# Eighteen weight-sum jobs in half 1 instead of twenty, two on VectorE beside the attention product, and a shorter preparation of half 2

## The chip, the cores and the metric

One core of a Trainium2 chip runs the whole program. TensorE (PE) multiplies matrices, VectorE (DVE), ScalarE (ACT) and GpSimd (POOL) work on tiles in on-chip memory, and SyncE (SP) issues transfers (DMAs); ACT and POOL issue some as well. Each engine takes its instructions in the order in which they stand, and waits where one isn't ready. Time is device time of one execution in microseconds (us); smaller is better.

## The reference

```
xn = layernorm(x)                               x: 2048 x 1024, f32
s  = linear attention of xn with wqkv (32 heads of 32), times wo
       phi(t) = where(t > 0, t + 1, exp(t)) + 1e-6
       o = phi(q) (phi(k)^T v) / (phi(q) sum(phi(k)) + 1e-6)
h  = silu(xn w1) * (xn w3)                      w1, w3: 1024 x 3584
out = x + s * silu(h w2)                        w2: 3584 x 1024
```

Both branches read xn.

## The kernel before

Every large product is made with fewer multiplications than the plain one, in f32 precision by three matmuls each (high times high, high times low, low times high, lines 109 to 111). So each operand is first split into a high part (ACT, line 103 or 474) and a low part (DVE, line 104 or 475).

**Halves.** The 2048 rows are worked on in two halves (`half(h)`). Half 1 (h = 0) makes keys, queries, then 14 pairs of hidden columns; half 2 (h = 1) makes keys and queries in turn, row products, then its 14 pairs. A pair is a gate gemm (`g0_8_` is that of pair 8 in half 1) and an up gemm (`u0_8_`). A gemm is seven products of 12 matmuls of 128x512, named by letter and operand: a with B11, b with T2, c with T3, d with T1, a again with B21, e with T4, d again with B22. They multiply the seven tiles A11, S2, S3, S1, A12, A22, S4 of the half's normalised rows, 2.1 MB each, always in that order. Half 2's seven tiles go into the places of half 1's, so each load (line 904, from `a_d`) waits until PE has done its last product with the old tile.

**Weights.** A pair's two weight blocks (1 MB each, line 442) go into two buffers in turn. Those of w1 and w3 are asked for by ACT, in its own instruction order, ahead of the cast of the block before; those of q and k by SP. All transfers of SP and ACT share eight completion semaphores in turn, so an issue waits until the transfer that had its semaphore before has landed.

**Side jobs.** `catch_up` is called after most products and lets one step of one side job be written there; `yield` ends a step. Side jobs, in this order: `prepare_next` (4 jobs: half 2's rows are normalised, transposed, combined and stored to `a_d`), then `weight_sums` (28 jobs): each loads eight blocks of w2 (line 1157), makes sums of them on POOL in three steps (11 instructions, tiles `w2s` and `w`, line 989) and stores them to `wt_d` by SP (line 1167), for the last product. Its tiles rotate through four buffers. `next_work` queues 20 of them in half 1, `attention_work` eight in half 2; what is left at the end of a half is written out at once. Every two pairs, sums of the hidden tiles (`hs`, `early_sums` and `later_sums`) go to POOL too, and to `h_d` by the queue in `stores_by`; while `later_sums` yields True, no weight sums step is written. ACT's next `h` tile (line 969) waits until these have read the old one.

**After half 2.** The attention product makes eight blocks of 256 rows, 84 matmuls each after the first (`tokens`): banks `as`, `bs`, `cs`, `ds`, emptied by DVE (lines 1455 to 1494), operands split one block ahead. Then the last product with h, `wt_d` and w2. A scheduler fixes the order of each engine from these program steps; `tc.issue_after` adds orders by hand.

Of the kernel before, what the change touches and what calls it, by code (L numbers as in the profile page):

```python
# [9 lines left out]
F32 = mybir.dt.float32  # L10
# [12 lines left out]
def tile_linear_attention_times_swiglu(  # L23
# [10 lines left out]
    nc = tc.nc  # L34
# [4 lines left out]
    NF = F // P  # L39
# [299 lines left out]
    def prepare_next(i):  # L339


        def turn(n, src):
            p_ = bank(f"t{n}1_{i}")
            for k in range(ND // 2):
                nc.tensor.transpose(p_[:, k * P:(k + 1) * P], src[:, k * P:(k + 1) * P], ident)
            return p_

        def steps(_):
            t = [job_tile([P, D], f"xn{i}_{e}") for e in range(2)]
            for c in range(2):  # L350
# [12 lines left out]
            bs = st.tile([P, 2, 2, nc.vector.BN_STATS_DIM], F32, tag="bs", name=f"bs1_{i}")  # L363
            for c in range(2):
                gather(t[c], bs[:, c])
                yield True
            spread(bs, m)
            yield True
            for c in range(2):
                normalise(t[c], m[:, c])  # L370
                yield True

            a11, a12, a21, a22 = (t[c][:, n * C:(n + 1) * C] for c in range(2) for n in range(2))
            keep_rows(1, i, "A11", t[0])
            keep_rows(1, i, "A22", a22)
            g = job_tile([P, 2, C], f"xg{i}")
            nc.vector.tensor_add(out=g[:, 0], in0=a21, in1=a22)
            yield True
            nc.vector.tensor_sub(out=g[:, 1], in0=a11, in1=a21)
            yield True  # L380
            keep_rows(1, i, "S1", g.rearrange("p n c -> p (n c)"))
            p_ = turn("A21", a21)
            nc.scalar.copy(out=a21, in_=p_)
            yield True
            yield True
            nc.vector.tensor_sub(out=g[:, 0], in0=g[:, 0], in1=a11)
            yield True
            nc.vector.tensor_sub(out=g[:, 1], in0=a12, in1=g[:, 0])
            yield True
            keep_rows(1, i, "S2", g.rearrange("p n c -> p (n c)"))  # L390
            p_ = turn("A11", a11)
            keep("A11", p_)
            nc.scalar.copy(out=a11, in_=p_)
            yield True
            p_ = turn("A12", a12)
            keep("A12", p_)
            nc.scalar.copy(out=a12, in_=p_)
            yield True
            p_ = turn("A22", a22)
            nc.scalar.copy(out=a22, in_=p_)  # L400
            yield True
            keep("A22", p_)
            yield True
            nc.vector.tensor_add(out=a22, in0=a21, in1=a22)
            yield True
            keep("S1", a22)
            yield True
            nc.vector.tensor_sub(out=a21, in0=a11, in1=a21)
            yield True
            keep("S3", a21)  # L410
            yield True
            nc.vector.tensor_sub(out=a11, in0=a22, in1=a11)
            yield True
            keep("S2", a11)
            yield True
            nc.vector.tensor_sub(out=a12, in0=a12, in1=a11)
            yield True
            keep("S4", a12)
            yield True

        return Job(lambda: None, steps)
# [163 lines left out]
    jobs = []  # L585
# [275 lines left out]
    def half(h):  # L861
        A = operand_tiles(h)

        def keys(pair, **how):
            return gemm(ops[f"k{h}_{pair}_"], A, uses[pair], **how)

        def run(g):
            for _ in g:
                pass

        def side_by_side(*gemms):
            for _ in zip_longest(*gemms):
# [12 lines left out]
        uses = [key_rows(h, pair) for pair in range(ND // 2)]  # L885
        if h == 0:
            early = [ops[f"k0_{pair}_"] for pair in range(ND // 2)]
            m = [keys(pair, early=True, own=pair == 0, led=pair == 0) for pair in range(ND // 2)]
            some = mybir.EngineType
            with tc.manual_schedule(engines={some.PE, some.Activation, some.DVE, some.Pool}):  # L890
                last = Opening(A, early, m).run()
            wide[0] = True
            for k in early[2:]:
                k.ask()
            early[2].then = early[3].next
        else:

            ops["q1_0_"].ask()
            for i, n in enumerate(AOPS):
                with ExitStack() as behind:  # L900
                    if i > 1:
                        behind.enter_context(tc.issue_after(ops["q1_0_"].asked.ins))
                    for k in range(ND // 2):
                        nc.sync.dma_start(out=A[n][:, :, k].bitcast(F32), in_=a_d[n][:, :, k])
        if h == 0:
            with tc.issue_after(last.ins):
                for g in m:
                    run(g)
        else:
            stores_by[0] = nc.gpsimd  # L910
            side_by_side(keys(0, paired=True), queries(0, paired=True))
            wide[0], stores_by[0] = True, nc.sync
            for pair in range(1, ND // 2):
                run(keys(pair))
                run(queries(pair))
            jobs.append((all_denominators(), False))
            for _ in row_products():
                pass
        jobs.append((attention_work(), False) if h else (next_work(), True))
        if h == 0:  # L920
            for pair in range(ND // 2):
                wide[0] = pair < ND // 2 - 1
                held[0] = 0 if wide[0] else HOLD
                run(queries(pair))
        wide[0] = False
        for pair in range(NF // 2):
            last = h < NH - 1 and pair == NF // 2 - 1
            gemms = [gemm(ops[f"{'gu'[e]}{h}_{pair}_"], A, use, paired=last) for e, use in enumerate(hidden(h, pair))]
            if last:
                side_by_side(*gemms)  # L930
            else:
                for g in gemms:
                    run(g)
        while jobs:
            run(jobs.pop(0)[0])
        if h:
            store_all()
            sums_by[0], stores_by[0] = nc.vector, nc.gpsimd

    def four_sums(x1, x2, s12, s34, e=nc.gpsimd):  # L940

# [127 lines left out]
    def later_sums(h, t, tiles, last):  # L1069
# [3 lines left out]
            keep_sums(h, t, q, pw0.tile([P, 2, 2, P], F32, tag="w0_6", name=f"hk{h}_{t}"))  # L1073
            yield True
        for i, _ in enumerate(steps):
            yield i < 6
            if last:
                yield True

# [64 lines left out]
        e.tensor_sub(out=b22, in0=b22, in1=b11)  # L1144
        e.tensor_sub(out=b21, in0=b21, in1=b22)

    def weight_sums(t, part, place=job_tile, queue=nc.sync):

        e = pool

        cols = slice(part * P, (part + 1) * P)

# [7 lines left out]
        def steps(r):  # L1160
            o1, o2 = (place([P, 8, P], f"w2s{t}_{part}_{i}") for i in range(2))

            def some(x, i, step):
                return x[:, i:i + step + 1:step]
# [12 lines left out]
            e.tensor_sub(out=o2[:, 3], in0=o1[:, 2], in1=r[:, 6])  # L1177
            e.tensor_sub(out=o2[:, 4:6], in0=some(r, 2, 3), in1=o1[:, 5:7])
            yield True
            e.tensor_sub(out=o2[:, 6:8], in0=some(o1, 4, 3), in1=r[:, 3:5])  # L1180
            store(8, o2)
            e.tensor_add(out=r[:, 0], in0=r[:, 1], in1=o2[:, 1])
# [4 lines left out]
        return Job(load, steps)  # L1187

    WSUMS = [(t, part) for t in range(NQ) for part in range(4)]
    NOW = 20  # L1190

    def next_work():

        yield from go_on([prepare_next(i) for i in range(TH // 2)])
        jobs.append((go_on([weight_sums(*w) for w in WSUMS[:NOW]]), "sums"))

    hm4 = const.tile([P, P // DH], F32, name="hm4")
    nc.vector.memset(hm4, 0.0)
# [171 lines left out]
    def attention_work():  # L1370
# [3 lines left out]
                work += key_values(k + e * (ND // 2)) + [j]  # L1374
        work += [divide(m, k) for m in range(2, S // (2 * P)) for k in range(ND // 2)]
        yield from go_on(work, 3)
        jobs.append((go_on([weight_sums(*w) for w in WSUMS[NOW:]]), "sums"))


    groups = []  # L1380
# [229 lines left out]
    jobs.clear()  # L1610
    pw0 = ctx.enter_context(tc.tile_pool(name="pw0", bufs=1, reuse_waits="tile"))

    ORDER = [p for chain in CHAINS for p in chain]
    STEPS = [(i, c) for i in range(len(ORDER)) for c in range(NCH)]
    OPENS, CLOSES = {c[0] for c in CHAINS}, {c[-1] for c in CHAINS}
# [157 lines left out]
```

## Time and profile before

| | |
|---|---|
| median of 3 runs | 2310.02 us (2305.24 to 2311.41) |
| profiled execution: time, span | 2305.8 us, 2304.0 us |
| busy share PE, DVE, ACT, POOL | 98%, 67%, 45%, 30% |
| mean granted TensorE clock | 0.995 |
| moved by DMA | 495.20 MB, 215 GB/s on the mean |
| weight sums on POOL | 472.7 to 1618.5 us (308 instructions, in both halves) |
| first matmul of half 2 | 748.0 us |

In rows of the profile stand the start and the duration in us, the engine, the line, the tiles as out<-in and a count; a bracket tells how long the engine had stood idle before and what ended it. An engine's name with q (SPq, ACTq) is its queue issuing a transfer; a row that begins "DMA" after the times is a transfer itself. Windows give busy us of each engine with the count of instructions, then the granted TensorE clock (1.00 is full), the share of the DMA engines and GB/s. A matmul's row shows a duration longer than the distance to the next, since matmuls overlap; counts in a window tell the rate.

### The profile page before, as it was taken

The numbers are of one execution on the slowest core, as the hardware profiler recorded it, in microseconds if no ns is written. First come the engines' busy times: TensorE is split into PE (matmuls) and PEld (weight loads), VectorE is DVE, ScalarE is ACT, GpSimd is POOL, SyncE is SP. The second block draws the span as 40 slices with busy tenths as digits, with TensorE's granted clock in tenths as the row PEclk, the third lists the DMA queues.
The fourth block names the chain that finished last, engine by engine and source line by source line (L and its number), as shares of the span: only waits on it lengthen the run. The fifth ranks groups of instructions, "written<-read, shape, count | busy, mean of one in ns | idle before, by whom it ended". The sixth has DMA issues, their size and how long they took to land.

```text
span 2304.0 us, 31463 instructions
## 1 busy us (share of the span) xinstructions
PE 2259.7 (98%) x10584; PEld 1847.6 (80%) x10584; DVE 1549.4 (67%) x2571; ACT 1041.8 (45%) x1778; POOL 702.6 (30%) x1171
## 2 busy tenths in 40 slices
PE   7999999999998899999999999999999999999998
PEld 6888888888877688777788888888888888888887
DVE  8987777666544686555866688865865555566576
ACT  6655544444332455433444444343623544444452
POOL 2220324367776522000332454477221000001010
PEclk9999999999999999999999999999999999999999
DMA  6555556577778745777765667777766756668595
GB/s 243 177 184 169 177 160 194 181 212 222 200 218 268 289 153 171 249 240 247 214 212 162 208 203 242 247 210 222 244 215 190 263 197 210 224 218 266 193 302 203
DMA packets 449842, 495.20 MB, mean 215 GB/s; under 512 B 23776, under 2 KB 348640, under 8 KB 449568
## 3 DMA queue, kind: packets, MB, share of 16 engines
q1 hardware_dynamic: 367136, 357.11, 49.4%
q0 software_dynamic: 24304, 77.35, 10.2%
q10 hardware_dynamic: 58240, 58.72, 8.2%
q8 instruction: 83, 1.36, 0.2%
q14 instruction: 79, 0.65, 0.1%
HBM read 315.62 MB, written 181.14 MB: 216 GB/s over the span
## 4 chain that ended last, share of the span: by engine, by line
PE 72%; DMA 12%; POOL 8%; DVE 3%; issue 3%; SPq 1%; ACT 1%; POOLq 0%; ACTq 0%; DVEq 0%
PE o L110 7%; PE o L111 7%; PE o L109 7%; POOL w2s L989 5%; DMA wt_d<-w2s 4%; POOL hs L989 2%; PE g L109 2%; PE g L110 2%; PE g L111 2%; DMA qd<-pq_d 1%; DMA xy<-y_d 1%; DMA wt_d<-w 1%; DMA qs_d<-qd 1%; PE trk L718 1%; DMA h_d<-h 1%
## 5 line engine op out<-in xcount | busy, mean ns | idle before, releaser
L109 PE MATMUL o<-w,l 128*128 128x512 f32 x728 | 283.2, 389 | 0.0
L110 PE MATMUL o<-w,l 128*128 128x512 f32 x728 | 283.2, 389 | 0.0
L111 PE MATMUL o<-w,l 128*128 128x512 f32 x728 | 283.2, 389 | 0.0
L103 ACT CAST l<-lr 128x896 fp32r<-128x896 f32 (+1 forms) x106 | 98.5, 931 | 202.9 <-PE o L111 113.3
L104 DVE TENSOR_TENSOR l<-lr,l 128x896 fp32r<-128x896 f32 (+1 forms) x106 | 113.5, 1072 | 81.7 <-ACT l L103 80.6
L109 PEld LDWEIGHTS o<-w,l 128*128 128x128 f32 x728 | 136.6, 188 | 28.5
L110 PEld LDWEIGHTS o<-w,l 128*128 128x128 f32 x728 | 136.6, 188 | 28.4
L111 PEld LDWEIGHTS o<-w,l 128*128 128x128 f32 x728 | 136.6, 188 | 28.3
L1568 POOL DMA_DIRECT2D out<-acc x14 | 12.0, 858 | 394.9 <-DVE acc L1566 394.9
L104 DVE TENSOR_TENSOR xy<-xy,xy 128x512 fp32r<-128x512 f32 x112 | 72.9, 685 | 67.5 <-ACT xy L103 67.2
L103 ACT CAST xy<-xy 128x512 fp32r<-128x512 f32 x112 | 64.9, 620 | 104.4 <-PE g L111 60.7
L1747 DVE TENSOR_TENSOR acc<-o,acc 128x512 f32<-128x512 f32 x64 | 43.7, 689 | 89.3 <-PE o L111 89.3
L110 PE MATMUL g<-xy,xy 128*128 128x512 f32 x224 | 87.7, 391 | 0.8 <-DVE xy L104 0.8
L111 PE MATMUL g<-xy,xy 128*128 128x512 f32 x224 | 87.2, 390 | 0.0
L989 POOL TENSOR_TENSOR w2s<-w 128x256 f32<-128x256 f32 x84 | 60.8, 738 | 81.5 <-DMA wt_d<-w2s 64.4
L109 PE MATMUL g<-xy,xy 128*128 128x512 f32 x224 | 82.8, 399 | 1.2 <-ACT xy L103 1.2
L989 POOL TENSOR_TENSOR hs<-h,hs 128x128 f32<-128x128 f32 (+1 forms) x130 | 75.4, 599 | 20.8 <-DMA h_d<-hs 17.5
L722 POOL DMA_DIRECT2D y_d<-y x48 | 34.9, 729 | 122.6 <-ACT y L746 67.1
L989 POOL TENSOR_TENSOR hs<-h,h 128x128 f32<-128x128 f32 x104 | 47.6, 479 | 74.3 <-DVE h L973 74.3
L104 DVE TENSOR_TENSOR w<-wr,w 128x512 fp32r<-128x512 f32 x98 | 62.9, 684 | 8.2 <-ACT w L103 8.2
L103 ACT CAST w<-wr 128x512 fp32r<-128x512 f32 x98 | 57.9, 620 | 17.7 <-DMA wr<-in_B_w 10.8
L989 POOL TENSOR_TENSOR w2s<-w,w2s 128x256 f32<-128x256 f32 x84 | 60.8, 739 | 0.0
(5625 smaller groups left out, 6869.6 us busy)
## 6 DMA issues: line engine op xcount, KB each, us to landing
lr<-h_d SPq DMA_DIRECT2D x102, 448.0 KB
wr<-wt_d SPq DMA_DIRECT2D x126, 256.0 KB
wt_d<-w2s SPq DMA_DIRECT2D x56, 512.0 KB
h_d<-hs SPq DMA_DIRECT2D x96, 256.0 KB
w<-in_B_w SPq DMA_DIRECT2D x112, 128.0 KB
xy<-x_d SPq DMA_DIRECT2D x28, 512.0 KB
xy<-y_d SPq DMA_DIRECT2D x28, 512.0 KB
wr<-in_B_w SPq DMA_DIRECT2D x56, 256.0 KB
```

What stands on the lines that cost most here:

```text
L103: nc.scalar.copy(out=hi, in_=src)
L104: return nc.vector.tensor_sub(out=lo, in0=src, in1=hi.bitcast(F32))
L109: nc.tensor.matmul(acc, lhsT=wh, rhs=ah, start=start, stop=False, skip_group_check=True)
L110: nc.tensor.matmul(acc, lhsT=wh, rhs=al, start=False, stop=False, skip_group_check=True)
L111: return nc.tensor.matmul(acc, lhsT=wl, rhs=ah, start=False, stop=stop, skip_group_check=True)
L718: nc.tensor.transpose(p_[:, t * P:(t + 1) * P], src[:, t * P:(t + 1) * P], ident)
L722: nc.gpsimd.dma_start(out=y_d[h][:, :, YS.index(n), pair], in_=t.rearrange("p (t d) -> p t d", d=P))
L989: self.last = getattr(self.e, name)(**how)
L1568: nc.gpsimd.dma_start(out=out[rows, cols], in_=a, accum_op=ALU.add)
L1747: nc.vector.tensor_add(out=a, in0=b, in1=a)
```

## The change

It alters four things. `prepare_next` has five `yield`s fewer in each of its four jobs. Half 1 gets 18 weight-sum jobs, of which those with an even part take four steps instead of three (`slow`), half 2 gets the next eight, and the last two are done by DVE in the catch-ups of the attention product, with tiles from the pool `pw0` and stores by POOL's queue. `later_sums` of the last pair holds weight sums back for all its steps. And hidden-tile stores go by POOL's queue from the last pair of each half on, through half 2's first gemms.

```
@@ prepare_next: five of these go
             nc.vector.tensor_add(out=g[:, 0], in0=a21, in1=a22)
-            yield True
             nc.vector.tensor_sub(out=g[:, 1], in0=a11, in1=a21)
...
@@ half
         else:
-            stores_by[0] = nc.gpsimd
             side_by_side(keys(0, paired=True), queries(0, paired=True))
             wide[0], stores_by[0] = True, nc.sync
...
         for pair in range(NF // 2):
+            if pair == NF // 2 - 1:
+                stores_by[0] = nc.gpsimd
...
-            sums_by[0], stores_by[0] = nc.vector, nc.gpsimd
+            sums_by[0] = nc.vector
@@ later_sums
-            yield i < 6
+            yield i < 6 or last
@@ weight_sums
-    def weight_sums(t, part, place=job_tile, queue=nc.sync):
-
-        e = pool
+    def weight_sums(t, part, place=job_tile, e=pool, queue=nc.sync, slow=False):
...
             yield True
+            if slow:
+                yield True
@@
-    NOW = 20
+    NOW, THEN = 18, 26
...
-        jobs.append((go_on([weight_sums(*w) for w in WSUMS[:NOW]]), "sums"))
+        jobs.append((go_on([weight_sums(*w, slow=w[1] % 2 == 0) for w in WSUMS[:NOW]]), "sums"))
...
-        jobs.append((go_on([weight_sums(*w) for w in WSUMS[NOW:]]), "sums"))
+        jobs.append((go_on([weight_sums(*w) for w in WSUMS[NOW:THEN]]), "sums"))
@@ before the attention product's blocks
+    def spare_place(i):
+        tags = iter((("w0_3", "w0_4", "w0_5"), ("l0", "w0_6", "w0_5"))[i % 2])
+
+        def place(shape, name):
+            return pw0.tile(shape, F32, tag=next(tags), name=name)
+
+        return place
+
+    jobs.append((go_on([weight_sums(*w, spare_place(i), nc.vector, nc.gpsimd) for i, w in enumerate(WSUMS[THEN:])], 1), "sums"))
```

How it stands in the order, at two places. First SP's queue at the passage from half 1 to half 2, where the tiles of half 2 (`A11_1`, `S2_1` and so on) and its first weights (`wk1_0`, `wq1_0`) are loaded; `wt_d4` rows are stores of weight sums, `h_d0` rows stores of hidden sums. Before:

```order
L904 DMA A11_1_7028<-a_dA11_139 128x2x512
L1167 DMA wt_d4_100<-w2s4_2_0_6747 128x8x128
L904 DMA A11_1_7028<-a_dA11_139 128x2x512 x3
L1036 DMA h_d0_87<-hs0_6_a_6778 128x4x128
L904 DMA S2_1_7029<-a_dS2_140 128x2x512 x4
L1036 DMA h_d0_87<-h0_12_0_6437 128x2x128
L1167 DMA wt_d4_100<-w2s4_2_1_6748 128x8x128
L1167 DMA wt_d4_100<-w2_4_2_6637 128x2x128
L1167 DMA wt_d4_100<-w2s4_3_0_6838 128x8x128
L442 DMA wk1_0__6949<-in_A_wqkv 128x8x256
L442 DMA wq1_0__6966<-in_A_wqkv 128x8x256
L904 DMA S3_1_7030<-a_dS3_141 128x2x512 x4
```

and after:

```order
L1161 DMA wt_d4_100<-w2s4_1_1_6320 128x8x128
L1161 DMA wt_d4_100<-w2_4_1_6221 128x2x128
L899 DMA A11_1_6986<-a_dA11_139 128x2x512 x4
L899 DMA S2_1_6987<-a_dS2_140 128x2x512 x4
L437 DMA wk1_0__6907<-in_A_wqkv 128x8x256
L437 DMA wq1_0__6924<-in_A_wqkv 128x8x256
L899 DMA S3_1_6988<-a_dS3_141 128x2x512 x4
L899 DMA S1_1_6989<-a_dS1_142 128x2x512 x4
L899 DMA A12_1_6990<-a_dA12_143 128x2x512 x4
```

The stores between the tiles and ahead of `wk1_0` are gone: the last weight sums of half 1 are stored ahead of the first tile, and the hidden sums of the last pairs stand in POOL's queue.

Second DVE in the attention product, at the end of block 3, where it empties the banks `cs_3`, `ds_3` and `as_3` and splits operands of block 4. Before:

```order
L1458 TENSOR_TENSOR s3_11_15876<-cs_3_15880,us_3_15877 128x512
L104 TENSOR_TENSOR XS2s_4_15845<-rS2q_4_15843,XS2s_4_15845 128x512
L1455 TENSOR_TENSOR s3_11_15876<-ds_3_15881,s3_11_15876 128x512
L104 TENSOR_TENSOR XS3s_4_15850<-rS3q_4_15848,XS3s_4_15850 128x512
L1494 COPY s3_00_15873<-as_3_15878 128x512
```

and after:

```order
L1454 TENSOR_TENSOR s3_11_15834<-cs_3_15838,us_3_15835 128x512
L104 TENSOR_TENSOR XS2s_4_15803<-rS2q_4_15801,XS2s_4_15803 128x512
L1451 TENSOR_TENSOR s3_11_15834<-ds_3_15839,s3_11_15834 128x512
L1163 TENSOR_TENSOR w2s6_2_0_15906<-w2_6_2_15901 128x256
L1164 TENSOR_TENSOR w2s6_2_0_15906<-w2_6_2_15901 128x256
L104 TENSOR_TENSOR XS3s_4_15808<-rS3q_4_15806,XS3s_4_15808 128x512
L1165 TENSOR_TENSOR w2s6_2_0_15906<-w2_6_2_15901,w2s6_2_0_15906 128x256
L1166 TENSOR_TENSOR w2s6_2_0_15906<-w2_6_2_15901,w2s6_2_0_15906 128x256
L1490 COPY s3_00_15831<-as_3_15836 128x512
```

Weight-sum instructions of the two moved jobs (`w2s6_2`, and `w2s6_3` further on) now stand between DVE's splits and the emptying of the banks, 22 of them in blocks 3 and 4.

More of the change, by code (lines that the diff above doesn't have):

```diff
@@ L384, in steps @@
             yield True
-            yield True
             nc.vector.tensor_sub(out=g[:, 0], in0=g[:, 0], in1=a11)
-            yield True
             nc.vector.tensor_sub(out=g[:, 1], in0=a12, in1=g[:, 0])
@@ L402, in steps @@
             keep("A22", p_)
-            yield True
             nc.vector.tensor_add(out=a22, in0=a21, in1=a22)
@@ L410, in steps @@
             keep("S3", a21)
-            yield True
             nc.vector.tensor_sub(out=a11, in0=a22, in1=a11)
```

## The prediction

> **What bounds the kernel now.** I read the totals first, then the span cut into windows, then who waits for whom on TensorE (PE), then the queues in the one place where PE waits.
>
> ```profile
> PE 2259.7 (98%) x10584; PEld 1847.6 (80%) x10584; DVE 1549.4 (67%) x2571; ACT 1041.8 (45%) x1778; POOL 702.6 (30%) x1171
> ```
>
> PE is busy for 98%, so only a place where PE stands idle, or runs at a lower clock, can be won. The windows find it (busy us and, in brackets, the count of instructions per engine; then granted clock, DMA share, GB/s):
>
> ```profile
> 600.00:720.00 120.00, 112.72 (x478) 91.27 (x478) 67.91 (x109) 47.39 (x87) 90.63 (x162) 0.97 0.73 210
> 740.00:760.00 20.00, 14.49 (x51) 10.78 (x51) 11.87 (x18) 5.92 (x11) 7.48 (x12) 0.83 1.05 363
> 760.00:780.00 20.00, 20.00 (x90) 16.40 (x89) 14.08 (x15) 4.41 (x8) 18.81 (x31) 1.00 1.05 392
> 780.00:800.00 20.00, 12.48 (x49) 9.24 (x49) 9.36 (x19) 10.61 (x18) 6.80 (x13) 0.83 0.53 185
> 1900.00:2000.00 100.00, 100.00 (x443) 82.81 (x442) 55.45 (x75) 43.22 (x62) 0.00 (x0) 1.00 0.68 225
> ```
>
> The last row is undisturbed: 100/443 = 0.2257 us a matmul. By that rate 600 to 720 holds 478 x 0.2257 = 107.9 us of work and loses 12.1; 740 to 760 holds 11.5 and loses 8.5; 780 to 800, with 8 small transposes among its 49 (about 1.1 us), holds 10.4 and loses 9.6. That is 30.2 us round the passage from half 1 to half 2 (PE begins half 2 at 748). PE's own waits there:
>
> ```profile
> PE trk L718 <- DVE pk L712: 6.0, 1, 6.0
> PE ak__7064 L109 <- ACT B11k__6968 L474: 4.6, 1, 4.6
> PE dg__6343 L109 <- ACT T2u__6466 L474: 3.5, 1, 3.5
> PE du__6530 L109 <- DVE cu__6529 L674: 2.0, 1, 2.0
> PE dk__7120 L109 <- DMA S<-a_dS: 1.5, 2, 1.0
> PE du__6159 L109 <- ACT T2g__6286 L474: 1.2, 1, 1.2
> ```
>
> **Stage 600 to 720.** PE waits there for operands that ScalarE (ACT) casts late. ACT's rows say why (a DMA row is ACT's queue issuing a weight load):
>
> ```profile
> 650.28 0.62 ACT L474 CAST B11g__6232<-wg__6039 128x512 fp32r<-128x512 f32 x1 [8.26 <-DMA h_d<-h]
> ...
> 672.70 0.38 ACTq L442 DMA_DIRECT2D wg__6412<-in_B_w  x1
> 673.12 0.62 ACT L474 CAST B11u__6416<-wu__6228 128x512 fp32r<-128x512 f32 x1 [10.79 <-DMA wt_d<-w2s]
> ...
> 684.36 0.63 ACT L969 ACTIVATE h<-c22g__6385 128x512 f32<-128x512 f32 x1 [6.62 <-POOL hs L989]
> ```
>
> The weight load stands in ACT's own order, and it waits for the landing of a store that SyncE (SP) issues: its completion semaphore is shared with that store. The store waits for GpSimd (POOL). So POOL's lateness holds ACT, and ACT holds PE: 8.26 us of it cost PE 1.2 (du__6159), 10.79 cost 3.5 (dg__6343). Is POOL late? The sums of hidden tiles (hs) of two pairs begin in the chain of waits at
>
> ```profile
> 594.80 1.68 POOL hs L989 x4
> ...
> 677.74 1.67 POOL hs L989 x4
> ```
>
> and in the same stretch before (511.67 is where the burst ahead began) all engines stood so:
>
> ```profile
> 511.67:594.80 83.13, 83.13 (x368) 68.86 (x367) 48.16 (x77) 31.89 (x58) 61.80 (x110) 1.00 0.75 217
> ```
>
> and POOL's instructions on w2s alone:
>
> ```profile
> 511.67:594.80 83.13, 40.01 (x67) 1.00 0.75 217
> ```
>
> Two pairs are 336 matmuls, 75.8 us of PE. POOL takes 83.1 us: 61.8 busy, 40.0 of it six weight-sum jobs of 11 instructions (6.67 us a job), and 21.3 idle, mostly waiting for its own stores to leave a tile (3.55 a job). It falls 7.3 us further behind with every two pairs, until PE pays.
>
> The order of the changed kernel has 55 weight-sum instructions where pairs 8 and 9 had 66: five jobs. 83.1 - 6.67 - 3.55 = 72.9 us, under 75.8: POOL keeps pace. Pairs 10 and 11 have 60, which makes 77.5 and one slip of under 2 us. The first sums stand three gemms of 84 matmuls earlier (up gemm of pair 5, not gate gemm of pair 7), the last in pair 12 instead of behind pair 13. Bounds of the gain here: 0 to 12.1 us. ACT's loads still wait on SP's stores, so I leave 2 us, above the 1.2 that an 8 us wait cost: **10.1 us won**.
>
> **First stall of half 2.** PE waited 4.6 us for the first key operand (ak__7064). ACT's last read of the buffer that its load goes into, and SP's queue before that load:
>
> ```profile
> 720.05 0.59 ACT L482 COPY sB22g__6926<-wg__6412 128x512 f32<-128x512 f32 x1
> ```
>
> ```profile
> 733.25 0.86 SPq L1167 DMA_DIRECT2D wt_d<-w2s  x1
> 734.55 3.16 SPq L1167 DMA_DIRECT2D wt_d<-w  x1
> 737.81 0.83 SPq L1167 DMA_DIRECT2D wt_d<-w2s  x1
> 738.74 2.60 SPq L442 DMA_DIRECT2D wk__6949<-in_A_wqkv  x1
> ```
>
> The second stall, below, in the chain of waits:
>
> ```profile
> 770.97 0.24 PE dk__7120 L111
> ...
> 772.95 13.28 DMA wk__7325<-in_A_wqkv
> ...
> 790.28 1.11 PE trk L718 x4
> ```
>
> The buffer was read out at about 721; the load left at 738.74, behind three stores of weight sums. In the changed order no store stands among the loads of half 2's A and S tiles, nor ahead of wk. It can leave some 17 us earlier, where 5 us would do: the 8.5 us go. What is late next would be the tiles: seven of 2.1 MB, each free when PE has done two products with it (24 x 0.2257 = 5.4 us, 387 GB/s asked, where the window at 760 moved 392). With wk and wq (2 MB, 5 us) the last tile lands about 11 us after PE's last product of half 1, and is first used ten products (27 us) into half 2. Bounds 0 to 8.5; **8.5 won**.
>
> **Second stall.** The next key load (wk__7325) may only leave when PE has ended dk (770.97), about 2.0 us later; then come its 13.28 us, then 4.05 us from landing (786.23) to trk, since in ACT's order pk stands behind the cast of that load. Meanwhile PE has four products (dq, two B21, dk's B22), 10.9 us. Stall = 2.0 + L + 4.05 - 10.9 = L - 4.9; with 13.28 that is 8.4, against 6.05 + 1.5 seen. The change keeps both orders; only L can change. It ran beside the late A and S tiles (DMA share 1.05); 11 us after half 1 they are in, 10 us before this load leaves. Loads of that size elsewhere:
>
> ```profile
> 1084.49 5.03 DMA wg__9700<-in_B_w
> ...
> 1116.40 7.11 DMA wu__10086<-in_B_w
> ```
>
> L of 5.03 to 7.11 leaves 0.1 to 2.2, 13.28 leaves all. I take 6.1, a stall of 1.2: **8.4 won**.
>
> The two windows lost 18.1 us for 12.1 of waits; the rest ran at granted clock 0.83, so a removed gap takes its slow matmuls along. [...]
>
> **What it adds.** Two jobs on VectorE (DVE): 7 x 0.414 + 4 x 0.282 = 4.03 us each, from
>
> ```profile
> L1003 DVE TENSOR_TENSOR hs<-h,h 128x128 f32<-128x128 f32 x8 | 1.9, 282 | 0.0
> L1005 DVE TENSOR_TENSOR hs<-h,hs 128x256 f32<-128x256 f32 x4 | 1.7, 414 | 0.0
> ```
> ```profile
> 1757.00:1776.00 19.00, 19.00 (x86) 15.73 (x85) 10.80 (x18) 6.68 (x13) 2.16 (x4) 1.00 0.74 223
> ```
>
> This is DVE's fullest block of the attention product after its start: 10.8 of 19 us. Fourteen of the 22 new instructions fall into one block, 5.1 us: 15.9 of 19. PE writes other banks meanwhile, so I take 0; bounds 0 and all 8.1. Behind the sums on DVE wait the adds that free the banks; each gets at most four instructions (1.7 us) more ahead of it.
> The two jobs' eight loads go on SP's queue ahead of operand loads that are needed about a block (19 us) later; the last four wait for a tile that a store must leave first. Cost 0 unless SP is held for that long. Their six stores, and the stores of each half's pair 12, move from SP to POOL, whose four instructions in the block above, issues of such stores, took 2.16 us of 19; some seven at the passage are 3.8 us, on an engine that has no weight sums left then: 0, at most 3.8.
> Preparation in 20 fewer steps (5 in each of 4 jobs) keeps its instructions. DVE's fullest part there:
>
> ```profile
> 200.00:240.00 40.00, 40.00 (x178) 33.14 (x177) 33.12 (x58) 21.04 (x36) 4.09 (x7) 1.00 0.50 146
> ```
>
> The order packs some 5% more DVE instructions into each gemm there: 34.8 of 40 us. Bounds 0 to 2; I take 0.3.
>
> Sum: 10.1 + 8.5 + 8.4 - 0.3 = 26.7 us. The profiled execution took 2305.8 us (span 2304.0), which gives 2279.1. The median of the three runs was 2310.02, 4.2 higher, which gives 2283.3. I forecast **2281 us**.
>
> **The rivals.**
> (1) The second stall stays: wk__7325's load is slow for itself and not for the tiles beside it. For it: at 772.95 all tile issues were over. Against: their bytes were not, by the DMA share. 2281 + 8.4 = 2289. Chance 0.14.
> (2) POOL stays late: its idle time is waiting for stores and may grow per job. 3 us more a job would use up the margin of 2.9 in 75.8. Then the first stage loses as before: 2291. Chance 0.12.
> (3) The change doesn't take effect at the passage: the tiles, now asked for earlier, fill the DMA engines so that wk lands as late as now. It would need wk in flight for some 25 us, against 13.28 for the slowest load seen. About 2307. Chance 0.07.
> (4) Slower: the weight loads on ACT now wait on nearer stores. In the new order the loads of pairs 8 and 10 wait on a store only 49 instructions ahead, 81 to 110 before, and the sums begin three gemms earlier. At the worst row a load costs PE 3.5 us, some 5 with its slow clock; it takes seven such loads of the fourteen between pairs 6 and 13 to undo 27 us and lose 7. This decides if POOL is as far behind at pair 8 as it now is at pair 12, three slips of 7.3 us. Against: up to 594.80 it had slipped twice and PE was whole (368 matmuls in 83.13 us is the clean rate). About 2318. Chance 0.05.
>
> The forecast keeps 0.62. If all 30.2 us go and runs fall at their fast end, 2272; rivals 1 and 2 in part together make 2297: this range leaves out (3), (4) and a little more. A difference under 0.3% (7 us, the runs' own spread is 6.2) could not be told from none. Faster by more: 0.62 + 0.14 + 0.12 = 0.88; within: 0.07; slower: 0.05.
>
> **What would show it.** First: hs bursts 76 us apart, no ACT wait over 7 us at a weight load in half 1, PE gaps under 2 us from 600 to the passage. Second: wk issued before PE's last product of half 1, and no PE wait on B11k. Third: the second key load lands within 7 us. In the attention product DVE near 16 of 19 us in one block, and PE whole. The forecast is wrong if the second key load still takes over 10 us, or if ACT waits as long for SP's stores with fewer jobs.

## The result, and the profile after

| | before | after |
|---|---|---|
| median, four runs each | 2308.35 us (2305.24 to 2311.41) | 2274.44 us (2272.63 to 2276.02) |
| profiled execution: time, span | 2305.8, 2304.0 us | 2276.0, 2274.2 us |

The ratio of the runs, after to before, is 0.9853 (95% interval 0.9836 to 0.9870): 34 us between the medians, 29.8 between the two profiled executions. The forecast was 2281 (2272 to 2297). The totals of the page, then the windows of before once more, on the kernel after:

```profile
PE 2247.8 (99%) x10584; PEld 1842.7 (81%) x10584; DVE 1555.3 (68%) x2593; ACT 1042.4 (46%) x1778; POOL 702.1 (31%) x1167
```
```profile
600.00:720.00 120.00, 120.00 (x531) 99.38 (x530) 73.04 (x114) 50.74 (x92) 77.01 (x136) 1.00 0.67 200
740.00:760.00 20.00, 20.00 (x90) 16.53 (x90) 10.63 (x13) 4.85 (x8) 18.91 (x32) 1.00 0.91 331
760.00:780.00 20.00, 18.39 (x88) 14.83 (x86) 14.25 (x28) 13.23 (x23) 8.85 (x14) 1.00 0.52 178
```

600 to 720 now holds 531 matmuls, not 478, which is the clean rate; between 740 and 780 only 1.6 us are missing, at full clock. TensorE's waits from 240 to 800 show what went, and four rows that were not there before:

```profile
PE trk L713 <- DVE pk L707: 1.6, 1, 1.6
PE du__3611 L109 <- ACT xn L394: 1.4, 1, 1.4
PE du__3234 L109 <- ACT T2g__3337 L469: 1.3, 1, 1.3
PE dg__3785 L109 <- ACT T2u__3905 L469: 0.7, 1, 0.7
PE du__2509 L109 <- ACT T2g__2615 L469: 0.6, 1, 0.6
```

These four lie between 260 and 420, where half 2's rows are prepared (`xn` and, further on, `xo` are tiles of that work). In the rows here and below `ak` to `dk` are products of a key gemm and `aq` to `dq` of a query gemm, `c22k` is a sum of key products, `pk` holds finished keys, and `trk` are TensorE's transposes of them. So that all kernels can be set side by side, this table gives the us that TensorE lost in each stretch: the distance from each matmul's start to the next, less the median for its shape (0.227 us for 512 columns), summed; e1 to e16 are the experiments below. Between 880 and 1120, the row products, shapes are mixed and a large part is no loss at all (the least is 13.5); only differences count there. Outside these stretches all kernels are alike to 0.5 us, save between 1120 and 1640, where they lose 5.8 to 9.0.

| kernel | 240 to 440 | 440 to 720 | 720 to 820 | 880 to 1120 | 1640 to 1800 | span |
|---|---|---|---|---|---|---|
| before | 0.2 | 11.8 | 19.1 | 17.1 | 0.0 | 2304.0 |
| after | 5.2 | -0.4 | 2.1 | 14.4 | -0.2 | 2274.2 |
| after, second profile (e15) | 3.1 | -0.4 | 4.1 | 15.1 | -0.2 | 2276.1 |
| e1 preparation back | 0.2 | -0.4 | 19.9 | 16.6 | -0.2 | 2290.3 |
| e2 preparation alone | 3.7 | 11.6 | 2.4 | 13.5 | -0.2 | 2284.2 |
| e3 no slower jobs | 2.1 | 12.4 | 1.0 | 14.7 | -0.2 | 2283.5 |
| e4 queue back | 4.7 | -0.4 | 2.2 | 14.7 | -0.2 | 2273.7 |
| e5 jobs alone | 0.2 | 12.3 | 8.5 | 15.9 | 0.4 | 2291.2 |
| e6 queue alone | 0.2 | 12.0 | 18.9 | 14.9 | 0.1 | 2300.2 |
| e7 more traffic | 3.6 | -0.4 | 16.0 | 15.1 | -0.2 | 2289.0 |
| e10 five on VectorE | 0.2 | 0.3 | 6.1 | 17.0 | 6.5 | 2282.6 |
| e11 four on VectorE | 0.2 | -0.1 | 2.2 | 16.9 | 1.3 | 2273.3 |
| e14 two tiles | 0.1 | -0.4 | 2.6 | 17.4 | -0.1 | 2273.6 |
| e16 two tiles, again | 0.1 | -0.4 | 2.3 | 16.6 | -0.2 | 2273.0 |

The change won 12.2 us in half 1 and 17.0 at the passage, lost 5.0 in the preparation, and won 2.7 at the row products and some 2.6 in small pieces elsewhere (1120 to 1640: 9.0 lost before, 6.4 after), of which no step of the prediction spoke: 29.5, against 29.8 between the spans.

Why half 1 is clean is seen on GpSimd. Its bursts of hidden sums, in the order of time, and a window from burst to burst:

```profile
512.61 0.88 POOL L985 TENSOR_TENSOR hs<-h,h 128x128 f32<-128x128 f32 x2
...
590.40 0.88 POOL L985 TENSOR_TENSOR hs<-h,h 128x128 f32<-128x128 f32 x2
...
662.18 0.88 POOL L985 TENSOR_TENSOR hs<-h,h 128x128 f32<-128x128 f32 x2
```
```profile
512.61:590.41 77.80, 77.80 (x345) 64.43 (x344) 47.21 (x74) 31.93 (x57) 58.08 (x103) 1.00 0.78 224
```

77.8 and 71.8 us apart, 74.8 on the mean, where they had been 83. GpSimd goes at TensorE's pace now; since its sums read TensorE's tiles, these rows show that it keeps up, and not how much time it has to spare. ScalarE's longest waits between 440 and 735, which had been 10.8 and 8.3 us at its weight operands (the first row sums six waits, 20.3 us before):

```profile
ACT h L965 <- POOL hs L985: 13.9, 6, 4.7
ACT B11u__4603 L469 <- DMA h_d<-h: 4.3, 1, 4.3
```

At the passage, SP's queue and the load behind the second stall in the chain of waits:

```profile
703.51 2.51 SPq L899 DMA_DIRECT2D A<-a_dA  x4
708.96 3.05 SPq L899 DMA_DIRECT2D S<-a_dS  x4
717.77 0.38 SPq L437 DMA_DIRECT2D wk__6907<-in_A_wqkv  x1
```
```profile
757.99 5.51 DMA wk__7283<-in_A_wqkv
```

The first key load left at 717.77, 21 us earlier than before, and the second landed in 5.5 us, not 13.3.

### The profile page after: what moved, and what is told of

The parts are those of the page before. It is cut to its first block, busy times and chain, and to the rows that moved or that the text cites. A ratio compares the mean times of both kernels' runs of the same rounds, so it can differ in the third digit from the quotient of the medians.

```text
span 2274.2 us, 31462 instructions
## 1 busy us (share of the span) xinstructions
PE 2247.8 (99%) x10584; PEld 1842.7 (81%) x10584; DVE 1555.3 (68%) x2593; ACT 1042.4 (46%) x1778; POOL 702.1 (31%) x1167
## 3 DMA queue, kind: packets, MB, share of 16 engines
q0 software_dynamic: 25680, 81.81, 10.8%
## 4 chain that ended last, share of the span: by engine, by line
PE 73%; DMA 7%; issue 4%; POOL 4%; DVE 3%; ACT 1%; SPq 1%; ACTq 0%; POOLq 0%; DVEq 0%
PE o L109 7%; PE o L111 7%; PE o L110 7%; PE g L109 2%; PE g L110 2%; PE g L111 2%; POOL hs L985 2%; DMA a_dA<-xo 1%; DMA qd<-pq_d 1%; POOL w2s L985 1%; DMA wt_d<-w2s 1%; DMA a_dS<-xo 1%; PE ds L110 1%; PE cs L110 1%; PE as L110 1%
## 5 line engine op out<-in xcount | busy, mean ns | idle before, releaser
L104 DVE TENSOR_TENSOR xy<-xy,xy 128x512 fp32r<-128x512 f32 x112 | 72.9, 686 | 62.5 <-ACT xy L103 62.2
L104 DVE TENSOR_TENSOR w<-wr,w 128x512 fp32r<-128x512 f32 x98 | 63.0, 685 | 11.6 <-ACT w L103 11.5
L103 ACT CAST w<-wr 128x512 fp32r<-128x512 f32 x98 | 57.9, 620 | 21.8 <-DMA wr<-in_B_w 15.1
```

What stands on the lines that cost most here:

```text
L103: nc.scalar.copy(out=hi, in_=src)
L104: return nc.vector.tensor_sub(out=lo, in0=src, in1=hi.bitcast(F32))
```

## The experiments

The change has four parts: A the shorter preparation, B fewer jobs in half 1 and two on VectorE, C the slower jobs, D the queue of the hidden stores. The first three kernels do one part alone, the next three leave one out. Each kernel was timed beside the kernel before, whose median was 2303.8 to 2305.3 in these comparisons, 3.0 to 4.5 us less than the 2308 from which theories start; a ratio is that to the kernel before, with its 95% interval.

The hold-back in `later_sums` has no kernel of its own. It is in the change and in all that start from it, and not in the three with one part alone. In the change it has nothing to hold back, since GpSimd ends its last weight sum of half 1 at 685.8 and the last pair begins at 697.9.

### Jobs alone (B)

```
# before, with
-    NOW = 20
+    NOW, THEN = 18, 26        # and the two jobs on VectorE, as in the change
```

> The kernel before with only the jobs changed: 18 in half 1 at the old rate, eight in half 2, the last two on VectorE in the attention product; preparation, the queue of the hidden stores and the rate are as before. The sums begin with pair 7 as before and all but one instruction stand ahead of the last pair's end, so no store of weight sums stands among the tiles. Theory: the passage's 17 us go, 600 to 720 loses its 10 to 12 us as before since the rate is the same, nothing is lost at 260 to 420, the two jobs on VectorE cost nothing: about 2291 (2288 to 2294). Rival (fewer jobs are enough everywhere): 2279 to 2281. Rival (VectorE's sums in the attention product cost up to 8 us): 2297 to 2299.

Measured: 2293.28 us, ratio 0.9950 (0.9938 to 0.9963). The time is the theory's (2288 to 2294), but partly by luck: 12 us were won of the 17 forecast, from a start 3 us lower. Half 1 lost its 12.3 as said and VectorE's sums cost 0.4 at most. The first stall went; the second stayed:

```profile
PE trk L718 <- DVE pk L712: 6.2, 1, 6.2
```

ScalarE's rows give two reasons. The cast of the second key load, issued at 764.23, began at 773.77, and pk behind it waited once more, for GpSimd's hidden sums:

```profile
773.77 0.62 ACT L474 CAST B11k__7306<-wk__7283 128x512 fp32r<-128x512 f32 x1 [7.56 <-DMA wk__7283<-in_A_wqkv]
776.51 0.63 ACT L708 ACTIVATE pk<-c22k__7140 128x512 f32<-128x512 f32 x1 [2.13 <-POOL hs L989]
```

So a GpSimd that comes late out of half 1 is felt at the passage without any store of weight sums among the tiles. TensorE read the old A11 last at 710.8, but ahead of the new one in SP's queue stood the last stores of weight sums, which waited for GpSimd until 714.15, and then hidden stores. So A11 left at 716.57, 5.8 us after that last read, where in the change it is 0.4. The tiles come later, and the key load runs beside them.

### Preparation alone (A)

```
# before, with five yields fewer in each prepare_next
```

> The kernel before with only the preparation shortened (20 steps fewer). Its 20 jobs keep the rate of six to two pairs, but begin in the up gemm of pair 5 and end in pair 12, so no store of weight sums stands among the tiles of half 2 or ahead of wk1_0. Theory: both stalls at the passage go (17 us), GpSimd still slips 7.3 us with every two pairs, so that some 8 to 12 us of waits stay, only earlier than 600 to 720, and 260 to 420 loses its 5 us: 2308 - 17 + 5 - 2, about 2294 (2290 to 2298). Rival (starting earlier gives GpSimd slack enough at any rate): the 12 us go too, 2282 to 2284. Rival (the stalls are due to the stores of hidden tiles on SP, which stay): 2308 to 2313.

Measured: 2283.96 us, ratio 0.9909 (0.9894 to 0.9924): 21 us, the largest gain of any part alone, and 10 us below the theory's centre, 3 of them by the lower start. By the table its places are as the theory has them: passage 2.4, half 1 still 11.6 (only earlier, at 533.97 and 606.19), preparation 3.7. The rest is mostly what the sum left out: 3.6 less at the row products, 2 less between 1460 and 1640. Why these shrank is open. The rival that an earlier start is enough is refuted:

```profile
PE cu__5105 L109 <- ACT T3u__5071 L469: 2.9, 1, 2.9
PE dg__5682 L109 <- ACT T2u__5805 L469: 2.1, 1, 2.1
PE trk L713 <- DVE pk L707: 2.0, 1, 2.0
```

### Queue alone (D)

```
# before, with the hidden-tile stores' queue as in the change
```

> The kernel before with only the queue of the hidden-tile stores changed (GpSimd's queue from the last pair of each half on). The stores of weight sums stay on SP between the tiles and ahead of wk1_0. Theory: the first stall stays, since the stores of weight sums wait for GpSimd and hold wk1_0, and 600 to 720 is ahead of the change: 2305 to 2311, no difference to tell. Rival (the hidden stores on SP are what holds the loads of the passage): 2290 to 2293.

Measured: 2302.16 us, ratio 0.9988 (0.9979 to 0.9997), 3 us below the theory's range and 3 us below the kernel before. The first stall's 4.6 us in one piece became 1.5, 1.3 and 2.3, and the second stayed at 6.6: the passage lost 18.9, as before; the 3 us come from the row products (2.2 less) and from between 1120 and 1640 (1.3 less). The stores of weight sums are enough to hold the loads, without the hidden ones.

### Preparation back (A undone)

```
# after, with the five yields of each prepare_next put back
```

> The changed kernel with the five yields of each preparation job put back; the 18 slower jobs in half 1, the two on VectorE and the moved stores stay. The preparation then ends three gemms later, and of the 198 weight-sum instructions of half 1 33 are left for its last pair and its end, whose stores stand in SP's queue among and behind the tiles of half 2 again, two of them ahead of wk1_0. Theory (the shortened preparation is what clears the passage, and it costs about 5 us of small waits between 260 and 420): those 5 us come back, 600 to 720 stays whole since the rate of sums is still five jobs to two pairs, and the first stall of half 2 (8.5 us) returns, perhaps with a late second key load (up to 8.4): 2278 to 2287, against 2274.4 as changed. Rival (the slower rate alone clears the passage, when the sums begin does not matter): the 5 us are won and nothing is lost, 2269 to 2270.

Measured: 2291.56 us, ratio 0.9943 (0.9931 to 0.9956), 4.6 us above the theory's upper end. The preparation's 5.0 us came back and half 1 stayed whole, since the slower rate is enough for that with the old start. But the passage lost 19.9, in one gap:

```profile
PE dk__7078 L109 <- issue: 17.3, 1, 17.3
```

SP's queue ahead of the second key load says where it began:

```profile
749.32 4.16 SPq L1166 DMA_DIRECT2D wt_d<-w2s  x2
753.57 5.96 SPq L1166 DMA_DIRECT2D wt_d<-w  x1
759.62 0.56 SPq L442 DMA_DIRECT2D wk__7283<-in_A_wqkv  x1
```

Three stores of the last weight sums, waiting for GpSimd, held the second key load until 759.62, though its buffer had been read out at 752. ScalarE's cast waited for that load, VectorE's low part for the cast, and behind that low part in VectorE's order stood the emptying of the bank (c22k, at 774.98) that dk writes next. The theory had put the stores ahead of the first key load; it was the second that they stopped, and VectorE's queue that turned it into 17 us. The hold-back in `later_sums` is in this kernel, and here sums are left for it to hold back (33 instructions); how much of the 19.9 us is due to it is open.

### No slower jobs (C undone)

```
-        jobs.append((go_on([weight_sums(*w, slow=w[1] % 2 == 0) for w in WSUMS[:NOW]]), "sums"))
+        jobs.append((go_on([weight_sums(*w, slow=False) for w in WSUMS[:NOW]]), "sums"))
```

> The changed kernel without the slower jobs: all 18 jobs of half 1 take three steps. They then run at six jobs to two pairs from pair 5 on and end in pair 11, so nothing of them is near the passage. Theory (GpSimd needs 83 us for two pairs with six jobs where TensorE needs 76, so it slips, and TensorE pays through ScalarE's weight loads): some 8 to 11 us are lost between 500 and 640, as with the shortened preparation alone (its windows 520 to 560 and 600 to 640 lost 5.2 and 5.8), and the passage stays clean: 2282 to 2285, against 2274.4. Rival (with 18 jobs that end two pairs earlier the slip never reaches TensorE): 2274 to 2276.

Measured: 2284.97 us, ratio 0.9911 (0.9896 to 0.9926), the upper end of the theory's 2282 to 2285. Half 1 lost 12.4 us again and the passage 1.0. ScalarE's rows show both ways in which GpSimd's slip arrives: by a store that holds a weight load, and by the sums that must have read a hidden tile before ScalarE writes the next:

```profile
529.65 0.63 ACT L965 ACTIVATE h<-c22g__4962 128x512 f32<-128x512 f32 x1 [8.97 <-POOL hs L985]
...
599.89 0.62 ACT L469 CAST B11u__5755<-wu__5567 128x512 fp32r<-128x512 f32 x1 [8.37 <-DMA wt_d<-w2s]
...
613.20 0.63 ACT L965 ACTIVATE h<-c22g__5724 128x512 f32<-128x512 f32 x1 [8.69 <-POOL hs L985]
```

TensorE stood still behind the 8.97 and the 8.69 (3.2 and 3.0 us), 1.1 behind the 8.37. The prediction showed a row of the second (6.62 us) and built on the first alone.

### Queue back (D undone)

```
# after, with the hidden-tile stores' queue as before
```

> The changed kernel with the queue of the hidden-tile stores as before (SP's queue in the last pair of each half, GpSimd's through half 2's first gemms). SP then issues the hidden stores of pair 12 and later ahead of and between the loads of the tile A11. Theory (it is GpSimd's lateness that makes such stores hold the loads, and with the slower jobs GpSimd is on time): 0 to 2 us lost, 2274 to 2277, the second key load lands within 7 us. Rival (these stores hold the tiles in any case, so the second key load leaves close behind the last tile and takes about 9 us, as with the jobs alone, where it left 7.4 us behind the last tile load and ScalarE's cast of it stood 9.5 us later): 2280 to 2283.

Measured: 2274.76 us, ratio 0.9866 (0.9848 to 0.9883), as the change itself. The key load took 5.59 us. Part D is worth nothing here once GpSimd is on time.

### More traffic at the passage

```
+                if self.name == "k1_1_":
+                    for n in spare_d:                # A11, S2, S3, S1
+                        nc.gpsimd.dma_start(out=spare_d[n], in_=spare[n].bitcast(F32))
```

> The changed kernel with 8.4 MB more to move at the passage: GpSimd's queue stores the tiles A11, S2, S3 and S1 of half 2 to a spare place in DRAM, two of them among its first stores of hidden sums of the last pair (about 740), two about 10 us later. By the 392 GB/s that the DMA engines moved at the passage these take about 21 us of all of them. Theory (the second key load is slow only where other transfers are still under way; the second stall is its landing time less 4.9 us): the load, which left at 758 and took 5.5 us, takes 9 to 13 us, and TensorE loses 4 to 8 us more there, some of it at a lower clock, or waits for the last tiles as well: 2279 to 2285. Rival (the load's time has to do with its own queue, not with other transfers): 5 to 7 us for the load, 2274 to 2276.

Measured: 2290.78 us, ratio 0.9938 (0.9926 to 0.9951): 16 us above the change, and 6 above the theory's end. The stores left at 714.0, 721.8, 745.4 and 753.3, two of them earlier than meant, and so both key loads were hit. The first, issued at 716.35, took 15.8 us to land where it took 7.0 to its cast in the change, though it left as far behind the last load of S2 (6.6 us for 6.4); what was added beside it were stores of GpSimd's queue. So the load's time does depend on transfers of other queues, and the rival falls. TensorE lost 7.8 us behind this load, before 760. The second key load, issued at 767.58, was cast 13.3 us later, but it also left only 2.4 us behind the last tile load, as in the kernel before, and so tells less. The extra stores kept half 2's last tile back as well, and TensorE waited for that (the longest piece in the chain after 735):

```profile
762.36 12.70 DMA S<-a_dS
```
```profile
760.00:780.00 20.00, 15.60 (x61) 11.69 (x59) 5.66 (x9) 3.79 (x5) 8.69 (x15) 0.86 1.03 380
```

### Four and five jobs on VectorE

```
# after, with the preparation's yields back, and
+    NOW, THEN = 16, 24   # only part 0 slower:  four on VectorE
+    NOW, THEN = 15, 23   # even parts slower:   five on VectorE
```

> The changed kernel with the preparation's yields put back, 16 jobs in half 1 (only those of part 0 slower, so about 5.5 jobs to two pairs, beginning with pair 7 and ending with pair 12), eight in half 2, and four on VectorE in the attention product: 24 of its 44 instructions fall into one block, where VectorE would need 19.6 of 19 us, and 12 into the next. Theory (the preparation's 5 us come back, GpSimd slips 2 us with every two pairs, which the start at pair 7 leaves too few of to be felt, the passage stays clean): 2269 to 2271. Rival (the full block on VectorE costs 1 to 4 us): 2271 to 2275. Rival (GpSimd's slip is felt again between 600 and 720): 2273 to 2278.

> The changed kernel with the preparation's yields put back, 15 jobs in half 1 (at the slower rate, beginning with pair 7 and ending with pair 12), eight in half 2, and five on VectorE in the attention product: 55 instructions instead of 22, of which 24 and 23 fall into two neighbouring blocks. By the rows of a block (10.8 of 19 us busy, 0.414 and 0.282 us an instruction) VectorE would need 19.6 and 19.2 of 19 us there. Theory (the preparation's 5 us come back, the passage stays clean, and VectorE's cover just about holds): 2269 to 2271. Rival (VectorE, full for two blocks, empties the banks late and TensorE waits 1 to 4 us a block): 2272 to 2278.

Measured: four 2276.82 us, ratio 0.9875 (0.9860 to 0.9891); five 2282.18, ratio 0.9900 (0.9883 to 0.9916). The first theory of each missed, and five took longer than its rival too; four lies where the rival of a slipping GpSimd puts it, but not by that way. In both the preparation lost nothing, half 1 stayed whole, and the attention product lost 1.3 and 6.5 us; the five had a longer second stall as well (4.0 us). But VectorE was not full, with five neither: it had 14.63 of 19 us (the third pair of numbers) round the longest wait, and 16.2 in its fullest 19.

```profile
1724.00:1743.00 19.00, 15.77 (x62) 12.27 (x61) 14.63 (x36) 4.14 (x7) 6.01 (x9) 0.91 0.82 261
```

VectorE's rows ahead of TensorE's longest wait, and that wait:

```profile
1737.02 0.43 DVE L1168 TENSOR_TENSOR w2s<-w 128x256 f32<-128x256 f32 x1 [2.81 <-DMA w<-in_B_w]
1737.36 0.42 DVE L1169 TENSOR_TENSOR w2s<-w 128x256 f32<-128x256 f32 x1
1737.69 0.42 DVE L1170 TENSOR_TENSOR w2s<-w,w2s 128x256 f32<-128x256 f32 x1
1738.03 0.42 DVE L1171 TENSOR_TENSOR w2s<-w,w2s 128x256 f32<-128x256 f32 x1
1738.36 0.69 DVE L1456 TENSOR_TENSOR s<-ds,s 128x512 f32<-128x512 f32 x1
```
```profile
PE ds L109 <- DVE s L1456: 2.4, 1, 2.4
```

VectorE stood idle for 2.8 us because the sums' own load had not landed, and the emptying of bank ds stood behind them. The load had left late: SP issued it from 1728.64 on, in its order behind an operand load that it held, by the profile for VectorE, until 1728.22. The job before had another such wait: its first load waited 3.5 us, until 1715.80, for the store of the tile that it goes into. The cost is a wait in a queue, not work; a share of busy time would never have shown it.

### Two tiles for the splits

```
             def keep(n, src):
+                o = outs[0]
+                outs.append(outs.pop(0))        # xo and, once free, xg by turns
                 split(o, src.rearrange("p (k s) -> p k s", k=ND // 2))
...
+            outs.append(g.rearrange("p n (k s) -> p n k s", s=P).bitcast(FR))
+            outs.reverse()
```

> The changed kernel with one thing more: in the preparation, the split tiles (xo) that are stored to a_d go by turns into xo and into the tile xg, which is free by then, so that a split no longer waits until the store before it has left. In the changed kernel ScalarE waited 53.9 us for such stores between 150 and 440 (21 waits), 32.9 us (16 waits) in the kernel before, with the same instructions, and TensorE lost 5.0 us between 240 and 440, and nothing there in the kernel before. Theory (the preparation in fewer steps cost TensorE 5 us because its splits now come closer together than a store takes to leave their one tile, and ScalarE's casts for TensorE stand behind them): ScalarE's waits on these stores fall under 25 us, the 5 us come back, 2269 to 2271, against 2274.4. Rival (it is VectorE's and ScalarE's work itself, packed closer, that is late): 2273 to 2276.

Measured: 2276.82 us, ratio 0.9880 (0.9865 to 0.9895). The time missed the theory's 2269 to 2271, but its mechanism is confirmed. ScalarE's waits for these stores between 150 and 440, in the changed kernel and then with two tiles:

```profile
ACT xo L103 <- DMA a_dS<-xo: 27.5, 11, 4.5
ACT xo L103 <- DMA a_dA<-xo: 26.4, 10, 5.3
```
```profile
ACT xo L103 <- DMA a_dA<-xo: 5.7, 3, 3.1
ACT xo L103 <- DMA a_dS<-xo: 5.4, 2, 3.6
```

53.9 us became 11.1, and TensorE's 5.2 became 0.1. Yet the time did not fall: in the profile the row products lost 17.4 where the change lost 14.4. To see whether that belongs to the kernel, both were run once more on one chip.

> The changed kernel once more, word for word, beside the one with two tiles for the splits, on one chip. Open is why the latter won the 5 us between 240 and 440 and was no shorter: in its profile TensorE lost 17.4 us between 880 and 1120 (by 0.2275 us a matmul of 512 columns), where the changed kernel lost 14.1, though the order of all engines there is the same. Theory (that difference belongs to one execution and not to the kernel): the loss between 880 and 1120 lies anywhere from 13.5 to 17.5 in this profile, and over the runs the two tiles win 1 to 4 us, so this kernel comes out 1 to 4 us longer than the other. Rival (it belongs to the kernel): 14.1 again to within 0.5 us, and this kernel is as long as the other or shorter, 2273 to 2276.

> The changed kernel with two tiles for the splits, once more, beside the changed kernel. Theory (its 3.3 us more between 880 and 1120 belong to one execution): the loss there lies anywhere from 13.5 to 17.5, and it is 1 to 4 us shorter than the changed kernel. Rival (they belong to the kernel: what is won ahead of half 2 is lost again at the row products): 17.4 again to within 0.5 us, and it is as long as the changed kernel or 1 to 3 us longer.

Measured: the change 2276.18 (2273.99 to 2277.87), ratio 0.9876 (0.9861 to 0.9891); two tiles 2275.06 (2274.80 to 2279.13), ratio 0.9878 (0.9861 to 0.9894). No difference. The losses between 880 and 1120 were 15.1 and 16.6, beside 14.4 and 17.4 the first time; between 240 and 440 the change lost 3.1 this time. By their words the theories came out and the rivals did not, since all four losses lie between 13.5 and 17.5 and neither came back to within 0.5; but the difference of the medians, 1.1 us, is within the noise. The pattern over all kernels speaks for the rival all the same: some 2 to 3 us of what two tiles win ahead are lost again at the row products, as in five of the six kernels with the old preparation (15.9 to 17.1; the other 14.9), though the order there is word for word the same. Why is open. No kernel tried is faster than the change by more than can be told.

## Why the prediction was right, and where it was not

The total came out: 26.7 us were predicted, and 34 were won between the medians at first, 29.8 between the profiled executions, 27.6 between the medians when the change was run again (e15). But it came out partly by luck, because two errors of about 5 us cancelled.

**Stage 600 to 720** (10.1 predicted): 12.2. GpSimd's lateness was the cause, as e1 (slower rate, whole) and e3 (old rate, 12.4 lost) show, and the step that counted five jobs to two pairs fits: 74.8 us between bursts for 72.9 to 77.5. The 2 us set aside for loads that wait on stores were not needed: the longest such wait was 4.3. The step knew one of two ways: hidden tiles that GpSimd has yet to read (e3) stop ScalarE as well. Rival (2) has an error: its 3 us more a job would be 15 us for five jobs, and 0.6 us a job are enough to use up the margin of 2.9, so the step had less to spare than it said.

**First stall** (8.5): all gone. e6, which leaves the stores of weight sums ahead of the loads and GpSimd late, keeps the loss; e2 and e5, where the sums end earlier, don't have it. Nor does e1, which has such stores but a GpSimd less late: there they stopped the second key load. The load left 21 us earlier, for 17 predicted.

**Second stall** (8.4, leaving 1.2): 1.6 us left, 2.0 in the second profile, where seven slow matmuls came with it. L was 5.51 for the 6.1 taken. The formula was 1.0 short, since the load left 2.8 us after dk, not 2.0 (VectorE's low part of B22k took 2.1 us). Rival (1), that this load is slow for itself, falls with the 5.51; that other transfers slow such a load is shown by e7. That the stall would go with the first one was right for the change, and wrong as a rule: e5 has the one without the other.

**VectorE's two jobs** (0): 0. The fullest 19 us with them had 13.91 us of work, for 15.9 predicted:

```profile
1690.00:1709.00 19.00, 19.00 (x86) 15.73 (x85) 13.91 (x35) 5.27 (x9) 6.88 (x10) 1.00 0.71 230
```

The argument by busy share happened to be right; e10 and e11 show that the danger was the sums' loads.

**Stores to GpSimd's queue** (0): 0, and no gain either (e4).

**Preparation** (0.3, bounds 0 to 2): this step failed. It cost 5.0 us (2.9 in the second profile; 1.9 to 5.0 in the six profiles with it). It priced VectorE's share of busy time; the limit was one tile, `xo`, from which a store must leave before the next split. The row was there to be read: ScalarE already waited 32.9 us for these stores in the kernel before, at no cost to TensorE. Twenty steps fewer made it 53.9, and ScalarE's casts for TensorE stood behind:

```profile
387.37 0.59 ACT L103 CAST xo<-tA 128x512 fp32r<-128x512 f32 x1 [4.04 <-DMA a_dA<-xo]
387.85 0.59 ACT L469 CAST T2g__3735<-sT2g__3733 128x512 fp32r<-128x512 f32 x1
388.71 0.59 ACT L394 COPY xn<-tA 128x512 f32<-128x512 f32 x1 [0.27 <-DVE xo L104]
```

**Not forecast:** 2.7 us at the row products and some 2.6 between 1120 and 1640. They made up for the preparation, and why they were won is open.

Rivals (2) to (4) did not come. The "some 5" us that (4) takes for a load with its slow clock are, at that row of the kernel before, 3.5 of wait and 1.7 in the eight slow matmuls behind it (granted clock 0.50 from 677.97 to 681.38). The parts don't add up: A, B and D alone give 21, 12 and 3 us, as much as the whole, and C, without which 10.5 are lost, is not among them; A and B both clear the first stall. Leaving out A costs 17 (with the hold-back in place), D nothing.

## What to carry to other kernels

When side work is moved to fewer steps, look for the tile that successive steps share: the waits that it already causes, free so far, show where packing the steps closer may cost (`xo`: 32.9 us of ScalarE's waits at no cost, then 53.9 at 5.0 us of TensorE's). A queue that serves loads and stores in one order hands one engine's lateness to all (in e1 three stores held a key load for 7.6 us after its buffer had been read out, and TensorE waited 17.3 us in the end); so bring that engine under the pace of the bound, here by one step more in every other job (74.8 us between GpSimd's bursts, where TensorE needs 75.8), and let its work end ahead of the loads that matter. Either alone left a stall here (e1 19.9 us at the passage, e3 12.4 in half 1). An engine with idle time is no sure cover for work that must wait for its own load, if the bound engine's buffers are emptied behind it (in e10 VectorE stood idle for 2.8 us, and TensorE waited 2.4).

## What the runs showed of the hardware

The second key load of half 2, 1 MB, took the longer in most of these kernels, the closer it left behind the last tile load of half 2 (time of issue to time of issue; the last column is to landing, or to ScalarE's cast in e1, e5, e7 and e10):

| kernel | apart | took |
|---|---|---|
| e7 | 2.4 us | 13.3 us |
| before | 3.1 | 13.3 |
| e6 | 4.2 | 12.2 |
| e5 | 7.4 | 9.5 |
| e1 (three stores between) | 11.5 | 8.3 |
| e2 | 13.5 | 5.7 |
| e10 | 13.8 | 8.0 |
| after | 14.0 | 5.5 |

The six kernels not listed, 10.9 to 14.5 us apart, took 5.6 to 6.5 us to the cast. From 3.1 to 7.4 us apart each us of distance took about 0.9 off, as if the load waited for the bytes ahead of it, though all issues are over: from 760 to 780 the share of the DMA engines was 1.05 in the kernel before and 0.52 in the change. Distance is not all: e10's load took 8.0 us with the tiles long in, by which its second stall was 4.0, and why is open.

The second thing is the granted clock. After lone gaps of TensorE up to 1.86 us (e16) no matmul was slow. After 1.98 (before and e15), 2.01 (e5) and 2.06 us (e2) seven ran at 0.43 us instead of 0.23; in the kernel before the granted clock was 0.50 there, from 701.86 to 705.27. After 1.99 (e2) and 2.14 us (e14) none did, and the clock stayed at 1.00 (e14, 760 to 770); after 2.3 us and more 6 to 13 did. So a gap of about 2 us cost 2 or 3.4 us in these runs (seven times 0.20 more); what decides between the two is not shown.
